# Tracing a routing step's row numbers and counts twelve steps later, and their stores three more

## The chip, the cores and the metric

One core of a Trainium2 chip runs the whole program. The metric is the time of one execution on the device in microseconds (us), taken outside the profiler; a profiled execution of the same kernel gives the trace. The engines are TensorE (PE), VectorE (DVE), ScalarE (ACT), GpSimd (POOL) and SyncE (SP), which here mostly issues DMAs. Each engine runs its instructions in the order in which the program holds them.

## The reference

Three layers follow each other. For 4 batches of 576 tokens, 8 heads of 64:

```python
def phi(x):                                # attention by 128 random features
    h = x @ omega.T - 0.5 * sum(x * x)
    return exp(h - max(h)) / sqrt(128)
kv  = einsum('bhsm,bhsd->bhmd', phi(k), v);  z = sum(phi(k), over s)
x   = einsum('bhsm,bhmd->bhsd', phi(q), kv) / (phi(q) . z + 1e-6)   # 2304 x 512

logits = x @ w_gate                        # 8 experts, w_gate 512 x 8
expert = argmax(logits);  gate = softmax(logits)[expert]
y = gate * (relu(x @ w1[expert]) @ w2[expert])       # 512 -> 1024 -> 512, one expert for a token

h = y @ w_in                               # 512 -> 2048
out = (h * sigmoid(1.702 * h)) @ w_out     # 2048 -> 512
```

## The kernel before, in words

The program goes over the batches. For each, the attention works in quads of four heads: k and q are loaded, transposed by DMA and multiplied by `omega` (`pr`); DVE takes row maxima (`small`), subtracts (`qp`, `kp`), ACT takes exponentials; `kv_ps` and `num` are the two products of the attention, and `xn` its normalized output. PE transposes `xn` (`tx`), and ACT and DVE split it into a high and a low part (`xh`, `xl`), since each exact fp32 product is made of three products of such parts. The attention of later batches is woven between the expert layer of earlier ones, so that the engines always have both kinds of work.

**Routing.** When a batch's attention is done, `route_steps(b)` runs. It makes the logits `lg`, their row maxima `rm`, a one-hot `oh`, exponentials `ex` and the gate. PE counts the one-hot over all tokens (`ct_ps`), and the expert with the largest count is `ci`, as an integer `es`. SP reads `es` into a register (`values_load`), and with it loads this one expert's weights (`st`) by DMA. The batch is then computed as if all its tokens went to this expert. ACT converts each piece of weights to its high part `wh`, and POOL (in places DVE) subtracts that for the low part `wl`. PE multiplies into PSUM tiles `m_ps`, of which there are two, ACT writes `h1h` from one and DVE `h1l`, and only then is its bank free for the next group of twelve products.

**The count.** The same function also does what is needed only if some token went to another expert: for each of the five blocks of 128 tokens a MAX (`lmx`) and a MAX_INDEX (`lix`) find the token's expert, `ixf` is that as a float, `cif` is the batch's expert as a float, `eq` compares the two, `hit` counts the agreements, `total` is lowered by them, and `rr` holds for each token an expert number and its gate, stored to `r_dram` by two DMAs on SP's queue. At the end of the program `total`, summed over the partitions on PE and cast to `tot_i`, decides whether a general path over `r_dram` runs. With these inputs it doesn't.

**Order.** The program is traced by Python generators that a merging loop advances in turn, so the text order is a weave; a scheduler then sets each engine's order by its own estimate of the times. The loop calls `tick()` once in each of its steps. `lag(n, fn)` puts `fn` off by n steps, and `flush()` calls all that is still waiting. `behind(ins, n)` keeps an instruction behind the n instructions that stand before it on its engine, without a wait.

After the four batches the last layer runs on PE nearly alone, its first weights having been prepared by DVE in between (`z`, from `raw_o`).

Of the kernel before, what the change touches and what calls it, by code (L numbers as in the profile page):

```python
# [8 lines left out]
F32 = mybir.dt.float32  # L9
# [3 lines left out]
U32 = mybir.dt.uint32  # L13
I64 = mybir.dt.int64
ACTF = mybir.ActivationFunctionType
ALU = mybir.AluOpType
AX = mybir.AxisListType
# [5 lines left out]
def kernel(  # L23
# [13 lines left out]
    nc = tc.nc  # L37
    B, H, S, D = q.shape
    M = omega.shape[0]
    E, DM, F1 = w1.shape  # L40
    F2 = w_in.shape[1]
    NT = B * S
    P = 128
    T = 4
    TAIL = S - T * P
# [63 lines left out]
    r_dram = dram.tile([NT, 2], F32, name="r_dram")  # L109
# [4 lines left out]
    def behind(ins, n):  # L114

        eng, me = ins.ins.engine, ins.ins.name
        found = [i for i in reversed(nc.cur_bb.bb.instructions) if i.engine == eng and i.name != me][:n]
        for x in found:
            tc.add_manual_dep(
                ins.ins, x.name,  # L120
                mybir.DependencyInfo(mybir.DependencyClass.NoSync, mybir.DependencyReason.DATA),
                reason="behind",
            )
# [44 lines left out]
    total = const.tile([P, 1], F32, name="total")  # L168
# [9 lines left out]
    def lag(n, fn):  # L178
        late.append((clock[0] + n, fn))
# [30 lines left out]
    att = tc.alloc_tile_pool(name="att", bufs=1)  # L210
# [289 lines left out]
    def route(b):  # L500
        g = route_steps(b)
        while True:
            with tc.high_priority() if b < HP_ROUTE else nullcontext():
                c = next(g, "end")
            if c == "end":
                return
            yield c

    def route_steps(b):
# [3 lines left out]
        for hf, tg in ((0, "n"), (1, "u")):  # L513
            c = slice(hf * HS, (hf + 1) * HS)
# [9 lines left out]
        for t in range(T + 1):  # L524
# [8 lines left out]
        lg = att.tile([P, T + 1, E], F32, tag="lg", name="lg", bufs=1)  # L533
# [10 lines left out]
            out=ex, in0=lg, in1=rm.to_broadcast([P, T + 1, E]), op=ALU.subtract  # L544
# [6 lines left out]
            out=ct_ps.rearrange("p t e -> p (t e)"), lhsT=ones, rhs=oh.rearrange("p t e -> p (t e)")  # L551
# [4 lines left out]
        ci = att.tile([P, 8], U32, tag="ci", name="ci", bufs=2)  # L556
# [4 lines left out]
        gate = att.tile([P, T + 1, 1], F32, tag="gate", name="gate", bufs=2)  # L561
# [4 lines left out]
        for t in range(T + 1):  # L566
            n = P if t < T else TAIL
            nc.scalar.activation(
                out=dg[:n, t * P:t * P + n], in_=ident[:n, :n], func=ACTF.Copy, scale=gate[:n, t, :]
            )  # L570
        cif = att.tile([P, 1], F32, tag="cif", name="cif", bufs=2)
        nc.vector.tensor_copy(cif, ci[:, 0:1])
        mx = att.tile([P, T + 1, 8], F32, tag="lmx", name="lmx", bufs=1)
        ix = att.tile([P, T + 1, 8], U32, tag="lix", name="lix", bufs=1)
        for t in range(T + 1):
            nc.vector.max(mx[:, t], lg[:, t])
            nc.vector.max_index(ix[:, t], mx[:, t], lg[:, t])
        ixf = att.tile([P, T + 1, 1], F32, tag="ixf", name="ixf", bufs=1)
        nc.vector.tensor_copy(ixf, ix[:, :, 0:1])
        eq = att.tile([P, T + 1, 1], F32, tag="eq", name="eq", bufs=1)  # L580
        nc.vector.tensor_scalar(out=eq, in0=ixf, scalar1=cif[:, 0:1], scalar2=None, op0=ALU.is_equal)
        nc.vector.memset(eq[TAIL:, T, :], 0.0)
        rr = att.tile([P, T + 1, 2], F32, tag="rr", name="rr", bufs=2)
        nc.vector.scalar_tensor_tensor(
            out=rr[:, :, 0:1], in0=eq, scalar=-float(2 * E), in1=ixf, op0=ALU.mult, op1=ALU.add
        )
        hit = att.tile([P, 1], F32, tag="hit", name="hit", bufs=1)
        nc.vector.tensor_reduce(out=hit, in_=eq.rearrange("p t o -> p (t o)"), axis=AX.X, op=ALU.add)
        nc.vector.tensor_tensor(out=total, in0=total, in1=hit, op=ALU.subtract)
        nc.vector.tensor_copy(rr[:, :, 1:2], gate)  # L590
        yield 0.5
        reg_t[b] = nc.values_load(
            es[0:1, 0:1], engines=[mybir.EngineType.SP], min_val=0, max_val=E - 1,
            skip_runtime_bounds_check_because="an index of the largest of E counts",
        )
        pump()
        nc.sync.dma_start(
            out=r_dram[b * S:b * S + T * P].rearrange("(p t) c -> p t c", t=T), in_=rr[:, 0:T]
        )
        nc.sync.dma_start(out=r_dram[b * S + T * P:(b + 1) * S], in_=rr[:TAIL, T])  # L600
        gb = moe.tile([P, S], F32, tag="gb", name="gb", bufs=2)
        g1 = pp.tile([P, T * P], F32, tag="u", name="g1", bufs=1)
        for t in range(T):
# [41 lines left out]
    def pump(n=0):  # L645
        ahead = 2 * NW - 1 if prep["split"] < 2 else NST
        while prep["staged"] < min(max(prep["split"] + ahead, 2 * NW - 1), 2 * NW * B) and prep["staged"] // (2 * NW) in reg_t:
            stage(*divmod(prep["staged"], 2 * NW))
            prep["staged"] += 1
        while n and prep["split"] < min(prep["free"], prep["staged"]):  # L650
            split_w(*divmod(prep["split"], 2 * NW))
            prep["split"] += 1
            n -= 1
# [310 lines left out]
    if True:  # L964
# [26 lines left out]
        while a_live:  # L991
            if force == "a" or (force is None and done_a - lead <= A_RATIO * done_m):
                c = next(A, "end")
# [5 lines left out]
            else:  # L999
                c = next(Mg)  # L1000
# [363 lines left out]
        p = hp.tile([P, SETW], F32R, tag="y2", name="p2", bufs=1)  # L1364
# [29 lines left out]
    with tc.If(more > 0), tc.tile_pool(name="gp", bufs=1) as gp:  # L1394
        with tc.For_i(0, NT // P, 1) as w:
# [21 lines left out]
            with tc.For_i(0, E, 1) as e:  # L1417
# [6 lines left out]
                with tc.If(cnt > 0):  # L1424
# [3 lines left out]
                    for f in range(NF1):  # L1428
                        wa = gp.tile([P, KD, P], F32, name="wa", bufs=2)
                        nc.sync.dma_start(  # L1430
                            out=wa,
                            in_=w1[bass.ds(e, 1), :, f * P:(f + 1) * P].rearrange(
                                "o (k p) f -> p (o k) f", p=P
                            ),
                        )
                        ps = pp.tile([P, P], F32, tag="m", name="g_ps", bufs=2)
                        for kk in range(KD):
                            nc.tensor.matmul(
                                out=ps, lhsT=wa[:, kk], rhs=xT[:, kk], start=(kk == 0), stop=(kk == KD - 1)
# [4 lines left out]
                    for dt in range(KD):  # L1444
                        wb = gp.tile([P, NF1, P], F32, name="wb", bufs=2)
                        nc.sync.dma_start(
                            out=wb,
                            in_=w2[bass.ds(e, 1), :, dt * P:(dt + 1) * P].rearrange(
                                "o (k p) d -> p (o k) d", p=P
                            ),  # L1450
                        )
                        ps = pp.tile([P, P], F32, tag="m", name="g_ps", bufs=2)
                        for f in range(NF1):
                            nc.tensor.matmul(
                                out=ps, lhsT=wb[:, f], rhs=ha[:, f], start=(f == 0), stop=(f == NF1 - 1)
# [53 lines left out]
```

## Time and profile before

| what | value |
|---|---|
| three runs | 767.16, 768.01, 770.99 us; median 768.01 us |
| the profiled execution | 765.51 us |
| its span in the trace | 763.5 us (the remaining 2.0 us lie ahead of and behind the recorded work) |
| busy: PE, DVE, ACT, POOL | 740.5, 533.3, 340.0, 132.3 us |
| granted clock of PE, mean | 0.995 of full speed |

Busy times are sums over one engine's instructions. An engine that is busy in nearly all of the span sets the time, if its work does not change; what it waits for in the rest is read from the waits and from the engines' rows in order of time.

### The profile page before, as it was taken

To read this page: it belongs to the slowest core of one execution; us is meant where nothing else is said; L and a number is where in the kernel's file an instruction comes from. 1 tells how busy PE (TensorE), PEld (TensorE's weight loads), DVE (VectorE), ACT (ScalarE), POOL (GpSimd) and SP (SyncE) were. 2 spreads that over 40 slices of the span, in tenths; PEclk is the share of its full clock that TensorE was granted. 3 is DMA by queue.
4 is the path that set the end of the run, shared out by engine and by line. 5 is a ranking of instruction groups with operands and counts; after the bars stand their busy time and mean duration, and the time that the engine had idled before them with its cause. 6 is when DMAs were issued, how large, how long until landed. Compare 5 with 4: busy or idle time off the path is not lost.

```text
span 763.5 us, 14425 instructions
## 1 busy us (share of the span) xinstructions
PE 740.5 (97%) x5589; PEld 717.1 (94%) x5589; DVE 533.3 (70%) x1188; ACT 340.0 (45%) x653; POOL 132.3 (17%) x78
## 2 busy tenths in 40 slices
PE   7998899999999999999999999999999999999997
PEld 6877799999999999989999999999999999999997
DVE  5877876686775686565979559981368777777774
ACT  5555573343533332233427564454576443444331
POOL 3564296538400441000000000000000000000000
PEclk9999899999999999999999999999999999999999
DMA  5447575258623553188255549972978544443311
GB/s 163 119 129 184 159 250 151 68 153 223 130 67 119 169 180 126 48 260 274 63 166 194 186 162 303 319 258 101 327 279 301 166 138 139 138 126 120 115 28 33
DMA packets 135852, 126.59 MB, mean 166 GB/s; under 512 B 57696, under 2 KB 120416, under 8 KB 134880
## 3 DMA queue, kind: packets, MB, share of 16 engines
q1 hardware_dynamic: 123936, 98.85, 43.6%
q10 hardware_dynamic: 11840, 26.74, 9.7%
q8 instruction: 46, 0.75, 0.4%
q14 instruction: 30, 0.25, 0.1%
HBM read 78.69 MB, written 40.39 MB: 156 GB/s over the span
## 4 chain that ended last, share of the span: by engine, by line
PE 82%; DVE 8%; DMA 4%; issue 3%; ACT 2%; SPq 1%; POOL 1%; ACTq 0%; POOLq 0%; DVEq 0%
PE m_ps L127 17%; PE qa L1213 13%; PE qa L1110 13%; PE qm L1213 7%; PE w_ps L127 4%; PE pb L1213 3%; PE qm L1110 3%; PE qu L1110 3%; PE num L433 3%; DMA st<-in_moe_w_dram 2%; PE kv_ps L391 2%; PE pr L333 2%; PE qn L1110 2%; PE qt L1110 2%; PE tq L419 1%
## 5 line engine op out<-in xcount | busy, mean ns | idle before, releaser
L1110 PE MATMUL qa<-y,wi 128*128 128x384 f32 x576 | 109.2, 337 | 0.4 <-DVE g L865 0.4
L1110 PEld LDWEIGHTS qa<-y,wi 128*128 128x128 f32 x576 | 101.4, 188 | 0.8 <-DVE g L865 0.8
L127 PE MATMUL m_ps<-xh,wh 128*128 128x288 f32 x256 | 78.5, 307 | 2.0 <-DVE h1l L699 2.0
L127 PE MATMUL m_ps<-xh,wl 128*128 128x288 f32 x256 | 76.1, 297 | 0.0
L127 PE MATMUL m_ps<-xl,wh 128*128 128x288 f32 x256 | 75.5, 295 | 0.0
L664 POOL TENSOR_TENSOR wl<-st,wh 128x1024 fp32r<-128x1024 f32 x23 | 55.6, 2424 | 92.7 <-ACT wh L662 87.5
L348 DVE TENSOR_REDUCE small<-pr 128x4 f32<-128x512 f32 (+1 forms) x80 | 51.1, 639 | 12.6 <-PE pr L340 5.0
L662 ACT ACTIVATE wh<-st 128x1024 fp32r<-128x1024 f32 (+1 forms) x33 | 33.9, 1033 | 53.3 <-DMA st<-in_moe_w_dram 37.4
L699 DVE SCALAR_TENSOR_TENSOR h1l<-m_ps,h1h 128x288 fp32r<-128x288 f32 x64 | 28.8, 452 | 33.2 <-ACT h1h L696 33.2
L127 PEld LDWEIGHTS m_ps<-xh,wh 128*128 128x128 f32 x256 | 48.1, 188 | 3.6 <-DVE h1l L699 3.2
L127 PE MATMUL m_ps<-h1h,wh 128*128 128x288 f32 x160 | 48.7, 305 | 0.7 <-DVE h1l L699 0.7
L127 PEld LDWEIGHTS m_ps<-xl,wh 128*128 128x128 f32 x256 | 48.1, 188 | 0.0
L127 PEld LDWEIGHTS m_ps<-xh,wl 128*128 128x128 f32 x256 | 48.1, 188 | 0.0
L696 ACT ACTIVATE h1h<-m_ps 128x288 fp32r<-128x288 f32 x64 | 25.7, 404 | 49.9 <-PE m_ps L127 47.6
L127 PE MATMUL m_ps<-h1l,wh 128*128 128x288 f32 x160 | 47.7, 299 | 0.0
L127 PE MATMUL m_ps<-h1h,wl 128*128 128x288 f32 x160 | 47.4, 297 | 0.0
L1213 PE MATMUL qa<-p,p 128*128 128x256 f32 x360 | 46.1, 282 | 1.1 <-DVE p L819 0.8
L1213 PE MATMUL qa<-p,gs 128*128 128x256 f32 x360 | 45.9, 282 | 0.0
L1213 PEld LDWEIGHTS qa<-p,p 128*128 128x128 f32 x360 | 44.1, 189 | 1.6 <-DVE p L819 1.0
L1213 PEld LDWEIGHTS qa<-p,gs 128*128 128x128 f32 x360 | 44.2, 189 | 0.0
L433 PEld LDWEIGHTS num<-kv,qpT 128*128 128x128 f32 (+1 forms) x320 | 36.2, 183 | 5.4 <-ACT qpT L421 2.7
L433 PE MATMUL num<-kv,qpT 128*128 128x65 f32 (+1 forms) x320 | 39.0, 265 | 2.3 <-ACT qpT L421 1.4
(212 smaller groups left out, 1830.7 us busy)
## 6 DMA issues: line engine op xcount, KB each, us to landing
g_dram<-g ACTq DMA_DIRECT2D x48, 384.0 KB, 3.9
st<-in_moe_w_dram SPq DMA_DIRECT2D x31, 512.0 KB, 4.6
pg<-g_dram SPq DMA_DIRECT2D x10, 1024.0 KB, 5.3
raw<-in_moe_w_in_dram SPq DMA_DIRECT2D x16, 512.0 KB, 3.9
gt<-g_dram SPq DMA_DIRECT2D x8, 1024.0 KB, 5.2
p<-wo_dram SPq DMA_DIRECT2D x6, 1024.0 KB, 7.1
yt<-y_dram SPq DMA_DIRECT2D x12, 384.0 KB, 5.9
vm<-in_v_dram SPq DMA_DIRECT2D x32, 128.0 KB, 3.0
```

Source lines behind the costliest of these rows:

```text
L127: ins = nc.tensor.matmul(out=ps, lhsT=a, rhs=b, start=start and n == 0, stop=stop and n == 2)
L333: nc.tensor.matmul(out=ps[:, :, h2], lhsT=xT[:, (2 * pr + h2) * 2 + t0 // 2], rhs=wbd)
L348: nc.vector.tensor_reduce(out=pm, in_=ps[:, :w], axis=AX.X, op=ALU.max, negate=on_act)
L391: nc.tensor.matmul(out=kv_ps[:, h, :], lhsT=kp[j // 2][:, j % 2, h2, :], rhs=vm[:, h, t, :], start=(t == 0), stop=False,)
L419: nc.tensor.transpose(tq[:, c, h2], qp[i][:, c, h2, :], ident)
L433: nc.tensor.matmul(out=ps[:n, c, h2, :], lhsT=lhsT, rhs=kv[:, h, :])
L662: nc.scalar.activation(out=hi[:, :, s], in_=st[:, :, s], func=ACTF.Copy)
L664: eng.tensor_tensor(out=lo[:, :, s], in0=st[:, :, s], in1=f32(hi)[:, :, s], op=ALU.subtract)
L696: nc.scalar.activation(out=hh[:, f], in_=ps, func=ACTF.Relu)
L699: nc.vector.scalar_tensor_tensor(out=hl[:, f], in0=ps, scalar=0.0, in1=f32(hh[:, f]), op0=ALU.max, op1=ALU.subtract)
L1110: ins = nc.tensor.matmul(out=ps, lhsT=w[:, a, ks], rhs=y[:, b, kk], start=start and kk + m == 0, stop=kk == 1 and m == 2, skip_group_check ...
L1213: ins = nc.tensor.matmul(out=ps, lhsT=x[:, f], rhs=w[i][:, f], start=start and f + m == 0, stop=f == NP - 1 and m == 2, skip_group_check=True,
```

## The change

In `route_steps(b)` the instructions from `cif` to the second column of `rr` move into a function `counted()`, which `lag(12, counted)` calls twelve steps later; the two stores to `r_dram` move into `rows()`, which is called three steps after that. `cif` and each MAX are kept behind the two DVE instructions that stand ahead of them where they are traced. No instruction is added or taken away, and `es`, the register load and the weights' DMAs stay.

```diff
-        cif = att.tile([P, 1], F32, tag="cif", name="cif", bufs=2)
-        nc.vector.tensor_copy(cif, ci[:, 0:1])
...
-        for t in range(T + 1):
-            nc.vector.max(mx[:, t], lg[:, t])
-            nc.vector.max_index(ix[:, t], mx[:, t], lg[:, t])
...
-        nc.vector.tensor_copy(rr[:, :, 1:2], gate)
         yield 0.5
         reg_t[b] = nc.values_load(
...
         pump()
-        nc.sync.dma_start(
-            out=r_dram[b * S:b * S + T * P].rearrange("(p t) c -> p t c", t=T), in_=rr[:, 0:T]
-        )
-        nc.sync.dma_start(out=r_dram[b * S + T * P:(b + 1) * S], in_=rr[:TAIL, T])
+
+        def counted():
+            cif = att.tile([P, 1], F32, tag="cif", name="cif", bufs=2)
+            behind(nc.vector.tensor_copy(cif, ci[:, 0:1]), 2)
...
+            for t in range(T + 1):
+                behind(nc.vector.max(mx[:, t], lg[:, t]), 2)
+                nc.vector.max_index(ix[:, t], mx[:, t], lg[:, t])
+            ixf = att.tile([P, T + 1, 1], F32, tag="ixf", name="ixf", bufs=1)
+            nc.vector.tensor_copy(ixf, ix[:, :, 0:1])
+            eq = att.tile([P, T + 1, 1], F32, tag="eq", name="eq", bufs=1)
+            nc.vector.tensor_scalar(out=eq, in0=ixf, scalar1=cif[:, 0:1], scalar2=None, op0=ALU.is_equal)
+            nc.vector.memset(eq[TAIL:, T, :], 0.0)
+            rr = att.tile([P, T + 1, 2], F32, tag="rr", name="rr", bufs=2)
+            nc.vector.scalar_tensor_tensor(
+                out=rr[:, :, 0:1], in0=eq, scalar=-float(2 * E), in1=ixf, op0=ALU.mult, op1=ALU.add
+            )
+            hit = att.tile([P, 1], F32, tag="hit", name="hit", bufs=1)
+            nc.vector.tensor_reduce(out=hit, in_=eq.rearrange("p t o -> p (t o)"), axis=AX.X, op=ALU.add)
+            nc.vector.tensor_tensor(out=total, in0=total, in1=hit, op=ALU.subtract)
+            nc.vector.tensor_copy(rr[:, :, 1:2], gate)
+
+            def rows():
+                nc.sync.dma_start(
...
+                nc.sync.dma_start(out=r_dram[b * S + T * P:(b + 1) * S], in_=rr[:TAIL, T])
+
+            lag(3, rows)
+
+        lag(12, counted)
```

Two places of the new order matter for what follows. The first is DVE behind the routing of batch 0, where the first groups of the expert layer run (`wl` and `h1l` are theirs; `rd`, `xn`, `xl`, `small`, `mx` and `qp` belong to the attention of the next batch). Before, these rows stood there:

```order
L438 RECIPROCAL rd<-rd 128x4
L444 TENSOR_TENSOR xn<-num,rd 128x2x128
L462 TENSOR_TENSOR xl<-small,xh 128x64
L699 SCALAR_TENSOR_TENSOR h1l<-m_ps,h1h 128x288 x2
L462 TENSOR_TENSOR xl<-tx,xh 128x512
L462 TENSOR_TENSOR xl<-small,xh 128x64
L348 TENSOR_REDUCE small<-pr 128x4
L357 TENSOR_TENSOR small<-small,sq 128x4
L357 TENSOR_TENSOR mx<-small,sq 128x4
L369 TENSOR_TENSOR qp<-pr,mx 128x512
L348 TENSOR_REDUCE small<-pr 128x4
L699 SCALAR_TENSOR_TENSOR h1l<-m_ps,h1h 128x288
```

Now the count stands among them. From the last MAX on the rows are (ahead of them, behind `xn`, stand `cif` and the other four pairs of MAX and MAX_INDEX):

```order
L584 MAX lmx<-lg 128x8
L707 SCALAR_TENSOR_TENSOR h1l<-m_ps,h1h 128x288
L585 MAX_INDEX lix<-lmx,lg 128x8
L587 CAST ixf<-lix 128x5
L589 TENSOR_SCALAR eq<-ixf,cif 128x5
L590 MEMSET eq 64x1
L707 SCALAR_TENSOR_TENSOR h1l<-m_ps,h1h 128x288
L592 SCALAR_TENSOR_TENSOR rr<-eq,ixf 128x5
L596 TENSOR_REDUCE hit<-eq 128x1
L462 TENSOR_TENSOR xl<-tx,xh 128x512
L462 TENSOR_TENSOR xl<-small,xh 128x64
L597 TENSOR_TENSOR total<-total,hit 128x1
```

The first `h1l` now has ten of the count's instructions ahead of it, and between the first and the third stand the last search, `ixf`, `eq` and its memset, `rr`, `hit` and `total`; behind `total` follow the reduction `small` and the other rows of before, up to the third `h1l`. The count came from the same engine's rows in batch 0's route, between the logits and `ct`, where these rows stood before:

```order
L543 TENSOR_TENSOR ex<-lg,rm 128x40
L577 MAX_INDEX lix<-lmx,lg 128x8
L576 MAX lmx<-lg 128x8 x4
L530 MEMSET lg_2056 128x16
L435 TENSOR_SCALAR rd<-num 128x4
L357 TENSOR_TENSOR small<-small,sq 128x2
L541 MEMSET oh 64x8
L577 MAX_INDEX lix<-lmx,lg 128x8 x2
L562 TENSOR_REDUCE gate<-ex 128x5
L577 MAX_INDEX lix<-lmx,lg 128x8 x2
L438 RECIPROCAL rd<-rd 128x4
```

From the two rows ahead of the same point (`ex`) on, the new order is:

```order
L348 TENSOR_REDUCE small<-pr 128x2
L540 TENSOR_TENSOR oh<-lg,rm 128x40
L543 TENSOR_TENSOR ex<-lg,rm 128x40
L435 TENSOR_SCALAR rd<-num 128x4
L357 TENSOR_TENSOR small<-small,sq 128x2
L541 MEMSET oh 64x8
L438 RECIPROCAL rd<-rd 128x4
L357 TENSOR_TENSOR mx<-small,sq 128x2
```

The MAX and MAX_INDEX are no longer among them. The second place is ACT at the end of the routing of batch 3, where `gb` is the gate, the table load and `wg<-total` prepare the last layer, and `wh_4380` is the first weight converted there. Before:

```order
L607 ACTIVATE gb<-g_3956 128x512
L608 ACTIVATE gb<-small 128x64
L926 DMA wo_dram<-z 128x4x256
L1014 ACT_TABLE_LOAD
L1014 ACTIVATE wg<-total 128x1
L908 DMA raw_o<-in_moe_w_out_dram 128x512 x2
L662 ACTIVATE wh_4380<-st 128x1024
L696 ACTIVATE h1h<-m_ps 128x288 x2
L662 ACTIVATE wh_4419<-st 128x1024
```

Now:

```order
L615 ACTIVATE gb<-g_3929 128x512
L616 ACTIVATE gb<-small 128x64
L934 DMA wo_dram<-z 128x4x256
L704 ACTIVATE h1h<-m_ps 128x288
L670 ACTIVATE wh_4380<-st 128x1024
L704 ACTIVATE h1h<-m_ps 128x288
L1022 ACT_TABLE_LOAD
L1022 ACTIVATE wg<-total 128x1
L916 DMA raw_o<-in_moe_w_out_dram 128x512 x2
L670 ACTIVATE wh_4419<-st 128x1024
```

One `h1h` has moved ahead of `wh_4380`, and the table load with `wg` has moved behind it. On DVE, `tot_i` stood between `total` and the first `wl` of that batch; now it stands behind that `wl` and one `h1l`. On SP the two `r_dram` stores stand a few issues later than before, in every batch.

## Rows read from the trace of the kernel before

**Rows 1.** The page's part 1, PE and the other engines: busy time, share, instructions.

```profile
PE 740.5 (97%) x5589; PEld 717.1 (94%) x5589; DVE 533.3 (70%) x1188; ACT 340.0 (45%) x653; POOL 132.3 (17%) x78
```

**Rows 2.** Busy time by stretch: PE, PEld, DVE, ACT, POOL, then PEclk, DMA, GB/s.

```profile
79.35:80.25 0.90, 0.15 (x4) 0.04 (x1) 0.90 (x4) 0.00 (x0) 0.90 (x1) 0.87 0.00 0
80.25:87.20 6.95, 6.20 (x39) 5.46 (x39) 6.44 (x48) 2.87 (x9) 0.36 (x1) 0.53 0.65 147
93.00:106.00 13.00, 13.00 (x110) 12.79 (x109) 8.28 (x21) 7.46 (x13) 9.43 (x4) 1.00 1.05 361
160.00:180.00 20.00, 20.00 (x170) 18.95 (x168) 12.20 (x37) 9.16 (x20) 10.71 (x6) 1.00 0.69 178
203.00:248.00 45.00, 45.00 (x394) 42.86 (x394) 29.08 (x112) 15.29 (x37) 2.37 (x1) 1.00 0.30 85
```

**Rows 3.** The chain that ended last, 78 to 110 us: start, length, piece.

```profile
79.43 0.08 DVE lmx L576
...
82.39 0.07 DVE ixf L579
...
82.94 0.62 PE ct_ps L550 x2
```

**Rows 4.** Timeline of SP's queue, 75 to 94 us: start, length, line, operation.

```profile
79.56 6.78 SPq L298 DMA_TRANSPOSE xT<-hl  x2
87.68 5.58 SPq L640 DMA_DIRECT2D st<-in_moe_w_dram  x8
```

**Rows 5.** Instructions on `lix`: duration in ns (min, median, max), first and last start.

```profile
L577 DVE FIND_INDEX8 lix<-lmx,lg x20: 154/161/171, 80.8 to 318.1; 128x8 uint32<-128x8 f32 x20
```

**Rows 6.** Timeline of ACT, 90.5 to 104 us, with idle time before in brackets.

```profile
90.66 1.19 ACT L662 ACTIVATE wh<-st 128x512 fp32r<-128x512 f32 x2
...
96.19 1.06 ACT L662 ACTIVATE wh<-st 128x1024 fp32r<-128x1024 f32 x1 [0.30 <-DMA st<-in_moe_w_dram]
97.15 0.39 ACT L696 ACTIVATE h1h<-m_ps 128x288 fp32r<-128x288 f32 x1
```

**Rows 7.** Timeline of PE, 90 to 108 us.

```profile
92.13 0.40 PE L127 MATMUL m_ps<-xh,wh 128*128 128x288 f32 x1
...
104.38 0.30 PE L127 MATMUL m_ps<-xh,wh 128*128 128x288 f32 x1
```

**Rows 8.** Timeline of DVE, 91 to 106 us.

```profile
95.92 0.23 DVE L462 TENSOR_TENSOR xl<-small,xh 128x64 fp32r<-128x64 f32 x1 [1.81 <-ACT xh L458]
97.58 0.46 DVE L699 SCALAR_TENSOR_TENSOR h1l<-m_ps,h1h 128x288 fp32r<-128x288 f32 x1 [1.43 <-ACT h1h L696]
99.03 0.46 DVE L699 SCALAR_TENSOR_TENSOR h1l<-m_ps,h1h 128x288 fp32r<-128x288 f32 x1 [1.00 <-ACT h1h L696]
...
102.72 0.45 DVE L699 SCALAR_TENSOR_TENSOR h1l<-m_ps,h1h 128x288 fp32r<-128x288 f32 x1
```

**Rows 9.** Timeline of POOL, 91 to 110 us.

```profile
95.85 9.51 POOL L664 TENSOR_TENSOR wl<-st,wh 128x1024 fp32r<-128x1024 f32 x4 [15.24 <-ACT wh L662]
```

**Rows 10.** `eq`: durations of all four; then DVE's timeline at batch 1.

```profile
L581 DVE TENSOR_SCALAR eq<-ixf,cif x4: 226/232/1682, 85.9 to 324.2; 128x5 f32<-128x5 f32 x4
...
163.80 1.68 DVE L581 TENSOR_SCALAR eq<-ixf,cif 128x5 f32<-128x5 f32 x1
...
166.25 1.41 DVE L584 SCALAR_TENSOR_TENSOR rr<-eq,ixf 128x5 f32<-128x5 f32 x1
```

**Rows 11.** Timeline of POOL at the same place.

```profile
163.07 2.38 POOL L297 TENSOR_TENSOR hl<-m,hl 128x1152 f16<-128x1152 f32 x1 [19.15 <-DVE cm L557]
165.53 2.11 POOL L256 TENSOR_TENSOR m<-m 128x1152 f32<-128x1152 f32 x1
```

**Rows 12.** Timeline of ACT and of PE at batch 3, 324 to 332 us.

```profile
325.29 1.28 ACT L1014 ACT_TABLE_LOAD   x1 [0.55 <-DVE hit L588]
...
328.41 1.06 ACT L662 ACTIVATE wh<-st 128x1024 fp32r<-128x1024 f32 x1 [1.62 <-DMA st<-in_moe_w_dram]
...
331.15 0.40 PE L127 MATMUL m_ps<-xh,wh 128*128 128x288 f32 x1 [0.66 <-DVE h1l L699]
```

More of the change, by code (lines that the diff above doesn't have):

```diff
@@ L570, in route_steps @@
             )
-        cif = att.tile([P, 1], F32, tag="cif", name="cif", bufs=2)
-        nc.vector.tensor_copy(cif, ci[:, 0:1])
-        mx = att.tile([P, T + 1, 8], F32, tag="lmx", name="lmx", bufs=1)
-        ix = att.tile([P, T + 1, 8], U32, tag="lix", name="lix", bufs=1)
-        for t in range(T + 1):
-            nc.vector.max(mx[:, t], lg[:, t])
-            nc.vector.max_index(ix[:, t], mx[:, t], lg[:, t])
[L578 to L585, printed above, removed]
-        )
-        hit = att.tile([P, 1], F32, tag="hit", name="hit", bufs=1)
-        nc.vector.tensor_reduce(out=hit, in_=eq.rearrange("p t o -> p (t o)"), axis=AX.X, op=ALU.add)
-        nc.vector.tensor_tensor(out=total, in0=total, in1=hit, op=ALU.subtract)
-        nc.vector.tensor_copy(rr[:, :, 1:2], gate)
         yield 0.5
@@ L596, in route_steps @@
         pump()
-        nc.sync.dma_start(
-            out=r_dram[b * S:b * S + T * P].rearrange("(p t) c -> p t c", t=T), in_=rr[:, 0:T]
-        )
-        nc.sync.dma_start(out=r_dram[b * S + T * P:(b + 1) * S], in_=rr[:TAIL, T])
+        def counted():
+            cif = att.tile([P, 1], F32, tag="cif", name="cif", bufs=2)
+            behind(nc.vector.tensor_copy(cif, ci[:, 0:1]), 2)
+            mx = att.tile([P, T + 1, 8], F32, tag="lmx", name="lmx", bufs=1)
+            ix = att.tile([P, T + 1, 8], U32, tag="lix", name="lix", bufs=1)
+            for t in range(T + 1):
[16 more added lines that the diff above has]
+                nc.sync.dma_start(
+                    out=r_dram[b * S:b * S + T * P].rearrange("(p t) c -> p t c", t=T), in_=rr[:, 0:T]
+                )
+                nc.sync.dma_start(out=r_dram[b * S + T * P:(b + 1) * S], in_=rr[:TAIL, T])
+            lag(3, rows)
+        lag(12, counted)
         gb = moe.tile([P, S], F32, tag="gb", name="gb", bufs=2)
```

## The prediction

> **What bounds the kernel now.** I read the page first: TensorE (PE) is busy for 97% of the span [rows 1], so the time moves only where PE waits, or where its clock is low. A table by stretches then shows where these places are. In 93 to 106 us and in 160 to 180 us PE is busy in every microsecond, while DVE has 8.28 of 13 and 12.20 of 20 [rows 2]. The weak place is 79 to 92 us, the routing of batch 0. PE does 0.15 us of work in the 0.90 us ahead of 80.25, and from 80.25 to 87.20 the granted clock is 0.53, about the lower level of 1.2 GHz [rows 2]. Last I read the chain of waits through that place, and DVE, ACT, POOL and PE in order of time around the place to which the change moves work. That the moved work is small is plain from its rows: the search for an index behind each MAX8 is 0.16 us [rows 5], the MAX8 about as long. The question is what each instruction waits for in its new place.
>
> **What leaves batch 0's route (79 to 93 us).** The chain goes through the count: from the first `lmx` at 79.43 to `ixf` at 82.39 there are seven pieces of it, 1.23 us in all, and behind them `xn` releases PE's `ct_ps` at 82.94 [rows 3]. Without them `ct_ps` and all behind it can start up to 1.2 us earlier. PE can't keep all of it, since the experts' weights bound what follows: SP's queue is in two transposing loads from 79.56 to 86.34, and the weights are issued from 87.68 [rows 4]. An earlier `es` passes neither. ACT converts the first two pieces of a weight from 90.66 for 1.19 us, so that the first is there at 91.26 [rows 6]; PE's first `m_ps` product stands at 92.13 [rows 7]. So the lead at 92 us is at most 0.9 us; call this term **-0.9** (0 to -0.9). The two stores of `rr` leave SP's queue from behind the weights' issues; nothing on PE reads what they write.
>
> **What arrives behind batch 0's route (94 to 105 us).** By the order rows, the count now follows `xn`, which ended at 94.1, and is mixed with the first two `h1l`. DVE idles 1.81, 1.43 and 1.00 us here [rows 8], 4.24 in sum. Five MAX8 and five searches at some 0.16 take 1.6 us and lie in the first two gaps, so they cost nothing as long as these gaps are there. The first `h1l` can't come earlier: it needs `h1h`, at 97.15 on ACT, and that stands behind a `wh` that begins at 96.19, when its weights land [rows 6]. So `h1l` ends at 98.04, the last search and `ixf` follow, and `eq` arrives at 98.2 to 98.5.
>
> There POOL is in the way. It runs four `wl` subtractions back to back from 95.85 for 9.51 us, 2.38 each, with ends at 98.2, 100.6, 103.0 and 105.4 [rows 9]. What POOL does to these small instructions is seen at batch 1: `eq` takes 1.68 us instead of its median 0.23 and ends at 165.48, `rr` takes 1.41 and ends at 167.66 [rows 10]; POOL's `hl` ends at 165.45, its `m` at 167.64 [rows 11]. Each came out as soon as POOL's instruction was over. `h1l`, which reads PSUM, isn't held: 0.46 us at 97.58 and at 99.03, both under `wl` [rows 8].
>
> So `eq` and `rr` each wait for an end of a `wl`; `total`, of a like form, has never met a POOL instruction in this trace. Four sums follow, by two open points.
> - `eq` gets through at 98.2, `rr` at 100.6. If `total` is held as well, to 103.0, what stands behind it by the order rows (two reductions, two small subtractions, `qp` and `h1l`, 2.8 us from the start of the first to the end of `h1l`, which is 103.17 today [rows 8]) put the end of the third `h1l` at 105.85. PE's fifth `m_ps` group needs the bank that it empties and starts at 104.38 today [rows 7]: **+1.5**. If `total` isn't held, +0.2.
> - `eq` misses 98.2 and gets through at 100.6, `rr` at 103.0. With `total` held to 105.4 the third `h1l` ends at 108.2: **+3.8**. Without, about 106.9: +2.5.
>
> PE runs its instructions in order and has the fifth group right behind the fourth, so this wait is lost; the lead from 92 us is eaten in it. The arrival is within 0.3 us of an end of a `wl`, which I can't settle, so I take the mean of the four, **+2.0**, and keep 0.2 to 3.8.
>
> The Trainium skill has this as a rule (SBUF — State Buffer, "Who interferes with whom"): DVE and GpSimd share one pair of SBUF ports as an exclusive lock, an instruction of DVE with two SBUF inputs contends with a GpSimd instruction that reads SBUF, and the one that comes second is fully blocked; one with at most one SBUF input outside the two-port modes is not. The held `eq` and `rr` and the free `h1l` agree with it. By this rule `total`, with two SBUF inputs, would be held too, and the term would be 1.5 or 3.8, with a mean of 2.65, and the time 770.4. No row of this trace shows `total` beside POOL.
>
> **Batch 1 (160 to 180 us).** The held `eq` and `rr` (1.45 and 1.25 us over their usual time) go from 163.8 to 167.7, and in their new place, some 4 to 10 us later, one or two of them probably wait for a `wl` again. PE had no idle time here with the hold [rows 2], so there is nothing to gain, and DVE has 7.8 us to spare in 20: **0** (-0.3 to +1).
>
> **Batch 2 (230 to 242 us).** From 203 to 248 us POOL has a single instruction of 2.37 us, DVE 29 of 45 us, and PE no idle time [rows 2]: **0**.
>
> **Batch 3 (323 to 332 us).** PE waits 0.66 us for `h1l` at 331.15, behind ACT's `wh` that waits 1.62 us for weights [rows 12]. In the new order one `h1h` more stands ahead of that `wh`, which can take away up to 0.66. Against it, the table load of 1.28 us, which lay in ACT's idle time at 325.29 [rows 12], now stands behind that `wh` and ahead of the next one. I take **-0.3**, between -0.7 and +0.6, the part of the load that its old cover leaves if half of it is uncovered.
>
> **Sum.** 765.5 (the profiled execution) + 2.0 + 0 + 0 - 0.3 = 767.2. The median of the runs is 768.0, 2.5 above the profiled one; with that, **769.7 us**.
>
> **Rivals.**
> - *Hidden.* `eq`, `rr` and `total` slip into the short gaps between two `wl`, or POOL's row of four has shifted, so that the third `h1l` ends by 104.3 as today. DVE's 4.24 us of idle time speak for it; against it, POOL's four stand without a gap [rows 9]. Then the lead of 0.9 stays: 768.0 - 0.9 - 0.3 = 766.8.
> - *Faster: the clock.* If the earlier `ct_ps` brings PE's full clock back early, or keeps it from falling, up to half of the 6.20 us of PE's work between 80.25 and 87.20 [rows 2] is won, 3.1 us, on top of the case before: 763.7. Against it: the clock falls at 80.25, when only one MAX8 of the count (0.08 us on the chain) has gone by. It decides if the fall is gone.
> - *Slower: a long stall and then the low clock.* `eq`, `rr` and `total` each wait for a `wl`, PE stands from 104.4 to 108.2, and the granted clock falls behind it as it did at 80.25, behind a stretch in which PE worked little. As the low stretch there cost 3.1 us, this gives 768.0 + 3.8 + 3.1 - 0.3 = 774.6. Against it: the stall ends before 106 in two of the four sums. It decides if PEclk falls anywhere behind 104.
>
> **Chances.** Held with a cost between 0.2 and 3.8: 0.50, its own range 767.9 to 771.5. Hidden: 0.20. Faster by the clock: 0.12. Long stall with low clock: 0.18. A measurement of this kernel can tell about 0.5%, 3.8 us, from no change: below 764.2 is faster, above 771.9 slower. The first case's upper end lies 0.4 below that bound and some of it (0.04) passes it. So faster 0.12, same 0.66, slower 0.22. The range leaves out the clock's gain and the upper part of the last case: 764.6 to 774.0.
>
> **What would show it.** Right: PE's `ct_ps` about 1.2 us earlier and `m_ps` at 91.3 to 92.1; `eq` and `rr` of batch 0 over 1 us long, each ending with a `wl`; PE idle 0.2 to 3.8 us for `h1l` near 104 to 108, at clock 1.00; at batch 1 no PE wait; less wait at 331. Wrong: `eq` and `rr` at 0.2 us near 98, or a PE wait in another place (a low clock behind 105, a later `wh` at batch 3).

## The result and the profile after

The changed kernel takes 777.71 us (median of six runs, 775.95 to 779.59) against 769.5 us of the kernel before on the same chip (six runs, 767.16 to 772.01): ratio 1.0105, 95% interval 1.0084 to 1.0127. It is slower by 8.2 us, outside the predicted range. One execution in a slower state, 786.45 us of the variant e7 below, is left out of all times and ratios. The page of the profiled execution (778.22 us) holds:

```profile
span 776.4 us, 14434 instructions
...
PE 743.2 (96%) x5589; PEld 719.4 (93%) x5589; DVE 541.3 (70%) x1188; ACT 340.4 (44%) x653; POOL 132.0 (17%) x78
```

PE's busy time rose by 2.7 us over [rows 1], though it runs the same 5589 products, and the span by 12.9 us over 763.5. That is more than the 8.2 us of the medians, since the profiled execution of before, 765.51 us, is one of its quick ones. Where the 12.9 us lie is seen in a table by stretches (PE, PEld, DVE, ACT, POOL, then PEclk, DMA share, GB/s) of after:

```profile
79.00:93.00 14.00, 11.67 (x111) 10.24 (x109) 12.79 (x59) 9.05 (x26) 1.55 (x2) 1.00 0.81 218
105.97:111.99 6.02, 6.02 (x35) 5.94 (x36) 4.35 (x14) 4.97 (x9) 3.04 (x2) 0.50 0.43 91
180.00:200.00 20.00, 15.78 (x125) 15.58 (x123) 11.04 (x34) 7.98 (x11) 12.34 (x6) 0.83 0.61 150
203.00:248.00 45.00, 45.00 (x408) 42.56 (x408) 31.25 (x101) 16.74 (x39) 4.78 (x2) 1.00 0.37 87
330.00:402.00 72.00, 66.60 (x489) 64.79 (x488) 49.30 (x108) 25.47 (x44) 0.00 (x0) 1.00 0.67 190
```

and of two of these stretches before:

```profile
180.00:200.00 20.00, 18.97 (x184) 17.95 (x184) 18.03 (x54) 10.58 (x19) 17.41 (x8) 1.00 0.78 194
330.00:402.00 72.00, 69.94 (x512) 68.98 (x512) 54.28 (x95) 24.62 (x42) 0.00 (x0) 1.00 0.59 183
```

**Batch 0.** The low clock of the routing, 0.53 in [rows 2], is gone in this execution (1.00 in 79 to 93). But then there is a new one, 0.50 for 6.02 us from 105.97. DVE's timeline ahead of it:

```profile
95.20 2.33 DVE L587 CAST ixf<-lix 128x5 f32<-128x5 uint32 x1
97.56 2.29 DVE L589 TENSOR_SCALAR eq<-ixf,cif 128x5 f32<-128x5 f32 x1
100.01 0.46 DVE L707 SCALAR_TENSOR_TENSOR h1l<-m_ps,h1h 128x288 fp32r<-128x288 f32 x1
100.38 1.92 DVE L592 SCALAR_TENSOR_TENSOR rr<-eq,ixf 128x5 f32<-128x5 f32 x1
103.02 0.15 DVE L597 TENSOR_TENSOR total<-total,hit 128x1 f32<-128x1 f32 x1
105.47 0.45 DVE L707 SCALAR_TENSOR_TENSOR h1l<-m_ps,h1h 128x288 fp32r<-128x288 f32 x1
```

POOL's at the same place:

```profile
92.79 9.49 POOL L672 TENSOR_TENSOR wl<-st,wh 128x1024 fp32r<-128x1024 f32 x4 [12.45 <-ACT wh L670]
```

and PE's:

```profile
89.38 0.38 PE L127 MATMUL m_ps<-xh,wh 128*128 128x288 f32 x1
...
90.57 0.40 PE L127 MATMUL m_ps<-xh,wh 128*128 128x288 f32 x1 [0.46 <-ACT wh L670]
...
105.97 0.61 PE L127 MATMUL m_ps<-xh,wh 128*128 128x288 f32 x1 [3.48 <-DVE h1l L707]
```

POOL's row is four subtractions of about 2.37 us, with ends near 95.2, 97.5, 99.9 and 102.3. `ixf`, `eq` and `rr` end at 97.53, 99.85 and 102.30: each was held until one of them was over. `h1l`, at 100.01 with 0.46 us under the last one, was not. The third `h1l` comes at 105.47, and PE begins its fifth group at 105.97 after 3.48 us without work: 1.59 later than in [rows 7], although its first `m_ps` product, at 89.38, was 2.75 earlier than there and the last product of the fourth group, at 102.20, still 2.05 earlier (before, 104.25). All of the place has moved: the first `h1l` stands at 94.56 in place of 97.58, POOL's row at 92.79 in place of 95.85. From the first `h1l` to the third it now takes 10.91 us, before 5.14. Behind the stall the clock is at its lower level, 1.2 GHz, for 6.02 us, which costs half of them, 3.0 us.

**Batch 1.** The chain that ended last (start, length, piece) shows the second place:

```profile
176.70 2.10 DVE ixf L587
...
179.95 0.16 DVE total L597
...
180.28 0.51 SPq L604
...
181.04 8.62 DMA st<-in_moe_w_dram
...
189.68 1.06 ACT wh L670
...
192.00 1.11 PE tq L419 x4
193.11 0.11 PE pr L339
...
199.27 0.06 PE pr L339
```

Here `ixf` takes 2.10 us (POOL's `wl` ends at 178.77), `rr` follows late, and the two stores of `rr` go out from SP's queue only at 179.88 and 180.28. Behind them stands the next weight, `st`. Its buffer came free at 178.77, with the end of that `wl`, but it is issued at 181.04, 2.27 us later, and lands 8.62 us after that. (Without the stores, in e4 below, the same load goes out 0.03 us behind the `wl`.) ACT converts it, `xl` stands on DVE behind ACT's `xh`, and PE waits 4.22 us (187.78 to 192.00). Then a `pr` product takes 0.11 us; at 199.27, with the clock back, 0.06. PE is busy for 15.78 us of 20 here, before for 18.97: 3.2 us lost by waiting. The low clock (0.50 from 192.00 to 195.24, 0.63 from there to 198.00) takes another 0.50 x 3.24 + 0.37 x 2.76 = 2.6 us.

**Batch 3.** PE is busy for 66.60 of 72 us, before for 69.94: 3.3 us lost, in four waits between 348 and 360 behind a weight that landed some 10 us after its issue at 340.37.

1.6 + 3.0 + 3.2 + 2.6 + 3.3 = 13.7 us, against 12.9 of the spans; a little comes back elsewhere (from 248 to 330 PE does 81.38 us of work, before 81.05). In 203 to 248 PE is busy throughout, as before.

### The profile page after: what moved, and what is told of

Its sections match the earlier page's. It is cut to its first block, busy times and chain, and to the rows that moved or that the text cites. A ratio compares the mean times of both kernels' runs of the same rounds, so it can differ in the third digit from the quotient of the medians.

```text
span 776.4 us, 14434 instructions
## 1 busy us (share of the span) xinstructions
PE 743.2 (96%) x5589; PEld 719.4 (93%) x5589; DVE 541.3 (70%) x1188; ACT 340.4 (44%) x653; POOL 132.0 (17%) x78
## 4 chain that ended last, share of the span: by engine, by line
PE 78%; DVE 9%; DMA 7%; ACT 2%; issue 2%; SPq 1%; POOL 0%; ACTq 0%; POOLq 0%; DVEq 0%
PE m_ps L127 16%; PE qa L1221 13%; PE qa L1118 13%; PE qm L1221 7%; DMA st<-in_moe_w_dram 5%; PE w_ps L127 3%; PE pb L1221 3%; PE qm L1118 3%; PE qu L1118 3%; PE num L433 3%; PE kv_ps L391 2%; PE qn L1118 2%; PE tq L419 2%; PE qt L1118 1%; PE pr L333 1%
```

## The experiments

Ratios are to the kernel before on the same chip, with 95% intervals. They need not equal the quotient of two medians, and the kernel before took 769.5, 768.95 (e1 to e4), 766.83 (e5 to e8) and 766.60 us (e9 to e12) beside them, so it is the ratios that can be compared. The experiments share one version of the changed function in which `LATE` holds the batches whose count is put off, `LAG_C` the steps for each, and `rows()` is called in the old place for the others; `LATE = (0, 1, 2, 3)` stands for the changed kernel, `LATE = ()` for the kernel before. An edit is shown against the changed kernel in this form. The scheduler sets the orders anew for each edit, so an edit can move more than it names; where the order of a trace decides a reading, it is said.

**One batch at a time.** The count and the stores late in batch 0, 1 or 3 alone:

```diff
-    LATE = (0, 1, 2, 3)
+    LATE = (0,)        # e1;  (1,) in e2;  (3,) in e3
```

> Only batch 0's count and stores are late; batches 1 to 3 as before. Theory (the loss has a part of its own in each batch): at batch 0 ixf, eq and rr are held by POOL's wl, PE waits some 3.5 us near 105 and then runs some 6 us at the half clock, while the half clock at 80 to 87 us is gone: in all 2 to 5 us slower than the kernel before, and no wait of PE for xl near 190. Rival (one cause, the late phase behind batch 0, brings the later waits with it): the wait near 190 comes as well, 6 us or more slower.

> Only batch 1's count and stores are late. Theory (the two r_dram stores wait on SP's queue for rr and hold the weights' issues behind them): PE waits 3 to 5 us near 183 to 190 for xl, behind a wh that waits for its weights; 3 to 7 us slower than before. Rival (batch 1 lost time in the full change only because batch 0 had shifted it): within 1 us of before.

> Only batch 3's count and stores are late. Theory (the raw_o loads of ACT's queue now stand behind a wh that waits for weights, land some 5 us later, and hold z, the next weights and h1l): PE loses 2 to 4 us between 330 and 402, 2 to 4 us slower than before. Rival (the loss there came from the shift of the earlier batches): within 1 us of before.

Measured: 777.02 us, 1.0111 (1.0081 to 1.0141) for batch 0; 770.58 us, 1.0028 (1.0009 to 1.0047) for batch 1; 770.36 us, 1.0021 (0.9996 to 1.0046) for batch 3. The parts do not add up: batch 0 alone loses all that the whole change loses, more than the 2 to 5 us expected, and without the wait near 190 that the rival asked for (PE is busy in all of 180 to 200). Its own stall is there (3.61 us for `h1l`, at 107.10), and a second one arises at batch 1, whose count stands where it stood before. DVE there:

```profile
169.69 1.79 DVE L586 TENSOR_SCALAR eq<-ixf,cif 128x5 f32<-128x5 f32 x1
171.64 2.02 DVE L589 SCALAR_TENSOR_TENSOR rr<-eq,ixf 128x5 f32<-128x5 f32 x1
174.25 1.72 DVE L594 TENSOR_TENSOR total<-total,hit 128x1 f32<-128x1 f32 x1
```

and POOL:

```profile
169.06 2.39 POOL L297 TENSOR_TENSOR hl<-m,hl 128x1152 f16<-128x1152 f32 x1 [20.65 <-ACT hl L296]
171.53 2.11 POOL L256 TENSOR_TENSOR m<-m 128x1152 f32<-128x1152 f32 x1
173.60 2.35 POOL L683 TENSOR_TENSOR wl<-st,wh 128x1024 fp32r<-128x1024 f32 x1
```

In [rows 10] the same `eq` and `rr` were held in the same way and cost nothing. Now the place comes 5.9 us later (169.69 for 163.80), POOL has a third instruction right behind the two, `total` is held too (each of the three ends with one of POOL's, at 171.5, 173.7 and 176.0), and PE waits 2.5 us for the `kp` behind it:

```profile
PE pr L339 <- DVE kp L369: 2.5, 1, 2.5
```

Behind this wait the clock is 0.50 from 177 to 183. So a hold that is free at one moment is not free at another, and a shift of one batch can bring it out in the next. Batch 1 alone showed a wait of 3.0 us for `xl` near 190 and clock 0.83 in 180 to 200, as in the whole change, but lost less than the 3 to 7 us expected. Batch 3 alone left PE busy for 67.65 of 72 us, and the third weight's conversion 7.0 us behind the second; the interval of its ratio holds 1. In that run's expectation I had named the order of the `raw_o` loads on ACT's queue as the cause; the next run keeps that order and not the loss, so that the order alone is not the cause.

**Without the stores.** The stores to `r_dram` are left out, in the changed kernel and in the kernel before (the general path, which doesn't run here, would find no rows):

```diff
-                lag(LAG_R, rows)      # e4, changed
...
-            rows()                    # e5, before
```

> The whole change, but the rows of expert numbers and gates are not stored (the general path, which does not run, would have nothing to read). Theory (stores hold SP's queue at batch 1): the wait of 4.2 us near 190 and the half clock behind it are gone or under 1 us, 4 to 6 us faster than the changed kernel, that is 2 to 4 us slower than before. Rival (POOL's hold of ixf and xl makes that wait, or the weights land late on their own): the wait stays at 3 to 5 us, 7 to 9 us slower than before.

> The kernel before without the stores of expert numbers and gates (left out as in the run of the whole change without them). Theory (the stores cost where they fall between a batch's weights, not as such; before, they stand right behind the first weights): 767 to 770 us, within 2 us of before. Rival (each pair of stores costs some us of DMA time wherever it stands): 4 to 8 us faster than before.

Measured: 767.67 us, 1.0001 (0.9983 to 1.0018), and 764.43 us, 0.9967 (0.9947 to 0.9987). With the changed kernel this makes a table of four (each against the kernel before on its own chip):

| | stores in their place | no stores |
|---|---|---|
| count and stores as before | 1 | 0.9967 |
| both late | 1.0105 | 1.0001 |

The right half of the second row is a clean comparison: up to 343 us DVE's instructions in e4 follow each other as in the changed kernel, but for one exchanged pair. So the late stores cost 1.0105 against 1.0001, some 8 us, as much as the whole loss; and this for 4 KB and 0.5 KB a batch, whose data no instruction of this run reads. The first row is not as clean. Up to 107 us e5 has DVE's order of before, from there on another; its `eq` and `rr` of batch 1, at 163.65 and 165.29, lie ahead of POOL's work (from 168.43) and are not held. So its 0.33% may be the order's, and what the stores cost in their old place is open. If it is 0.33%, two thirds of the loss come from the stores' new place; if it is nothing, all of it. Batch 0's stall is still there in e4 (3.6 us for `h1l`), but PE is busy in all of 180 to 200 and for 71.20 us in 330 to 402. In ACT's timeline at batch 3 the third weight of the list follows the second like this in the changed kernel:

```profile
340.81 1.04 ACT L670 ACTIVATE wh<-st 128x1024 fp32r<-128x1024 f32 x1
...
350.46 1.06 ACT L670 ACTIVATE wh<-st 128x1024 fp32r<-128x1024 f32 x1 [6.42 <-DMA st<-in_moe_w_dram]
```

and like this without the stores:

```profile
334.03 1.05 ACT L680 ACTIVATE wh<-st 128x1024 fp32r<-128x1024 f32 x1
...
338.43 1.06 ACT L680 ACTIVATE wh<-st 128x1024 fp32r<-128x1024 f32 x1 [1.17 <-DMA st<-in_moe_w_dram]
```

9.65 us against 4.40.

**The stores on another queue.** All stays as in the changed kernel, but ACT's queue issues the two stores. Is it SP's queue that stands still behind the stores (they wait for `rr`), or do the writes themselves hold the transfers up?

```diff
-            nc.sync.dma_start(out=r_dram...
+            nc.scalar.dma_start(out=r_dram...
```

> The whole change, with the two stores of each batch issued from ACT's queue in place of SP's. Theory (on SP's queue they wait for rr and hold the weights' issues and data behind them): PE's wait of 4.2 us near 190 is under 1.5 us and the time 768 to 773 us. Rival (the small stores themselves slow all DMA that is under way, whichever queue issues them): the wait stays at 3 us or more, 775 to 779 us.

Measured: 772.47 us, 1.0080 (1.0052 to 1.0108). The wait at batch 1 is gone (PE busy in all of 160 to 200). There the first load now goes out 0.02 us behind POOL's `wl` (which ends at 178.97), ahead of the first store, which ACT issues at 179.35:

```profile
178.99 0.38 SPq L659 DMA_DIRECT2D st<-in_moe_w_dram  x1
```

So it has neither the queue's wait nor the writes ahead of it, and this place doesn't tell the two apart; the next run does. At batch 3 the loss stayed (66.71 of 72). ACT issues the stores at 331.92 and 332.31 and two `raw_o` loads at 332.88 and 333.46, SP a weight at 334.19:

```profile
331.92 0.36 ACTq L599 DMA_DIRECT2D r_dram<-rr  x1
...
333.46 0.44 ACTq L927 DMA_DIRECT2D raw_o<-in_moe_w_out_dram  x1
...
344.08 1.06 ACT L681 ACTIVATE wh<-st 128x1024 fp32r<-128x1024 f32 x1 [6.50 <-DMA st<-in_moe_w_dram]
```

The view of the DMAs from 331.5 to 344 us has the bytes moved in 40 slices of 0.31 us, and below it the loads with their KB and the median us from issue to landing:

```profile
GB/s 184 23 23 13 13 0 2 0 39 39 223 13 0 0 0 13 131 79 26 26 13 105 249 419 420 420 419 446 364 357 406 354 338 351 354 370 357 226 89 69
raw_o<-in_moe_w_out_dram ACTq DMA_DIRECT2D x2, 512.0 KB, 7.4
st<-in_moe_w_dram SPq DMA_DIRECT2D x2, 512.0 KB, 9.1
```

From 334.2 on three loads of 512 KB are open on two queues, and yet little is moved until 338.1 but for a few slices; then they run at 340 to 450 GB/s. So loads issued behind these small stores waited for some 4 to 5 us, on SP's queue too, which held no store of `rr`.

**Larger rows.** Are the short rows the reason? Each store writes whole rows of 512 bytes, padded with zeros, to a wider tensor in DRAM, in the same place and waiting for the same `rr`:

```diff
-            rr = att.tile([P, T + 1, 2], F32, tag="rr", name="rr", bufs=2)
+            rr = rw_t[b][:, 0:2 * (T + 1)].rearrange("p (t c) -> p t c", c=2)
...
-            nc.sync.dma_start(out=r_dram[...], in_=rr[:, 0:T] ...)
+            nc.sync.dma_start(out=rw_dram[b * 2], in_=rw_t[b])
```

(`rw_t[b]` is 128x128 and zeroed by POOL beforehand; the second store is changed alike, and `r_dram` is not written.)

> The whole change with the same two stores at the same places on SP's queue, still waiting for rr, but each partition's row is padded to 512 bytes (the general path, which does not run, would have to read them at other addresses). Theory (writes of 8 and 32 bytes hold up the transfers behind them for some us): the weights land about 5 us after their issue behind the stores, as without stores, PE's wait near 190 is under 2 us, and the time is 768 to 772 us. Rival (SP's queue, which waits for rr, is what holds the weights): the wait near 190 and the loss between 330 and 402 stay, 775 to 779 us.

Measured: 770.44 us, 1.0035 (1.0013 to 1.0058), two thirds of the loss gone with 16 and more times the bytes; DVE's order is that of the changed kernel but for a few exchanged neighbours. SP's queue waits as before: POOL's `wl` ends at 182.42, and the load goes out behind the stores 2.22 us later (2.27 in the changed kernel), lands 5.41 us after that in place of 8.62, and PE waits 1.1 us for `xl` in place of 4.2:

```profile
183.91 0.48 SPq L605 DMA_DIRECT2D rw_dram<-rr  x1
184.64 0.40 SPq L662 DMA_DIRECT2D st<-in_moe_w_dram  x1
```

and among PE's waits (total, times, longest):

```profile
PE tq L420 <- DVE xl L463: 1.1, 1, 1.1
```

So of the 4.2 us the queue's wait alone leaves 1.1. In 330 to 402 PE is busy for 70.73 us of 72. The DMAs of the 6.5 us behind the first store at batch 1, in the changed kernel:

```profile
GB/s 0 17 9 0 0 1 2 0 0 0 63 101 164 227 50 0 0 0 0 0 0 0 0 0 6 132 170 57 25 13 25 25 0 25 32 57 158 227 221 284
st<-in_moe_w_dram SPq DMA_DIRECT2D x2, 512.0 KB, 8.8
```

and with the wide rows:

```profile
GB/s 0 0 161 230 13 0 66 133 3 0 76 221 246 132 145 239 246 403 277 290 347 364 299 330 339 364 365 340 378 372 365 381 347 301 109 60 113 139 365 391
st<-in_moe_w_dram SPq DMA_DIRECT2D x2, 512.0 KB, 5.1
```

Weights land in 8.8 us behind the short rows and in 5.1 behind the wide ones; in the corresponding 6.5 us without stores (e4) in 3.8. The Trainium skill (DMA: Bandwidth & Descriptors, Specifications) has 512 bytes as the least transfer for full rate and says that a smaller one is a read, a change and a write. The runs agree in so far as rows padded to this length hold the loads behind them less, 5.1 against 8.8 us; no other length was tried, and no run shows the read and the change. Why the short rows hold up others, and not only themselves, is open.

**A quiet place for batch 0's count, then for batch 1's too.** If the hold by POOL is what costs at batch 0, a place without POOL gives the gain of the shorter route without the stall.

```diff
-    LATE = (0, 1, 2, 3);  LAG_C = (12, 12, 12, 12)
+    LATE = (0,);          LAG_C = (60, 12, 12, 12)     # e7
+    LATE = (0, 1);        LAG_C = (60, 45, 12, 12)     # e8
```

> Only batch 0's count and stores are late, and by 60 steps in place of 12, so that they fall into the stretch near 130 to 160 us where GpSimd has nothing to do; batches 1 to 3 as before. Theory (late is good for batch 0's route, and only POOL's hold at 95 to 105 spoils it): ixf, eq, rr and total at 0.15 to 0.25 us each, no wait of PE near 105, full clock at 80 to 87 and at 105 to 112; 2 to 5 us faster than before. Rival (any later place loses, since DVE, ACT and DMA of the next route are pressed): the time stays within 2 us of before or above it.

> As the run with batch 0's count 60 steps late, and batch 1's 45 steps late as well (it falls behind 200 us, where GpSimd is idle too). Theory: the hold of eq and rr at batch 1 (2.7 us of DVE before) goes as well; PE had no wait there, so it is the same as the other within 1.5 us, 2 to 5 us faster than before. Rival (what stands behind batch 1's route decides): PE waits near 180 to 190 for xl or kp, and the time is 3 us or more above the other.

Measured: 780.44 us, 1.0154 (1.0077 to 1.0231; three runs, 773.44, 780.44 and 783.41) for batch 0 alone, 764.16 us, 0.9980 (0.9959 to 1.0001) for both. The first is the opposite of what was expected; the second is, by its interval, hardly told apart from the kernel before. In both the count of batch 0 stands near 150 us and is not held. In e8 POOL has no instruction from 148 to 158, and DVE shows:

```profile
152.21 0.16 DVE L584 CAST ixf<-lix 128x5 f32<-128x5 uint32 x1
152.41 0.23 DVE L586 TENSOR_SCALAR eq<-ixf,cif 128x5 f32<-128x5 f32 x1
```

PE is busy in all of 160 to 200 there, at clock 1.00, and for 70.51 of 72 in 330 to 402; the longest wait for `h1l` is 0.9 us. e7, which left batch 1's count in the old place, is slower than the change itself. Its longest waits of PE:

```profile
PE w_ps L127 <- ACT h1h L715: 7.9, 3, 3.9
PE pr L339 <- DVE kp L369: 2.0, 1, 2.0
```

The 2.0 us for `kp` lie behind batch 1's count, which is partly held by POOL again, as in e1. The 7.9 us for `h1h` lie at 296, 334 and 364 us and are not settled: weights that land late stand ahead of the first two, and stores in the old place beside the second, but which shift brought them together was not tried.

**The hold taken away where it arose.** The stores are left out as in e4, and DVE makes the low parts of batch 0's first five weights instead of POOL:

```diff
-    SPLIT_D = (0,)
+    SPLIT_D = (0, 1, 2, 3, 4)
```

> The whole change without the stores (left out), and with batch 0's first five weight pieces subtracted on DVE in place of GpSimd, so that nothing runs on GpSimd where batch 0's count stands. Theory (GpSimd holds ixf, eq and rr): these take 0.15 to 0.25 us each, and PE's wait of 3.6 us for h1l near 105 falls below 2 us (DVE has some 5 us more to do there); 762 to 768 us. Rival (the count's mere place between the first h1l makes the wait): it stays above 3 us, 768 us or more.

Measured: 764.29 us, 0.9976 (0.9957 to 0.9995), against 1.0001 of e4: taking POOL away at batch 0 gives 0.25%, 1.9 us, about as much as the two intervals together leave open; the traces are plainer. DVE and POOL at the place of the count:

```profile
102.57 0.17 DVE L584 CAST ixf<-lix 128x5 f32<-128x5 uint32 x1
103.85 1.17 DVE L586 TENSOR_SCALAR eq<-ixf,cif 128x5 f32<-128x5 f32 x1
105.60 0.17 DVE L589 SCALAR_TENSOR_TENSOR rr<-eq,ixf 128x5 f32<-128x5 f32 x1
```

```profile
102.62 2.37 POOL L682 TENSOR_TENSOR wl<-st,wh 128x1024 fp32r<-128x1024 f32 x1 [21.95 <-ACT wh L680]
```

`ixf` began 0.05 us ahead of POOL's subtraction and takes 0.17 us; `eq`, which meets it, is held to its end at 104.99; `rr` behind it is free. PE waits 1.1 us in place of 3.6, and its clock stays at 1.00 from 79 to 112.

**The best of both.** The count of batches 0 and 1 in the quiet places, and `rr` kept in SBUF for all batches and stored only inside the general path (e11); and the kernel before with the latter alone (e12). Both compute all of the reference.

```diff
-            rr = att.tile([P, T + 1, 2], F32, tag="rr", name="rr", bufs=2)
+            rr = rr_c[b]                  # one tile for each batch
...
-        rows()                            # per batch
...
+            for b in range(B):            # in the general path only
+                nc.sync.dma_start(out=r_dram...[b], in_=rr_c[b]...)
```

> Batches 0 and 1 with the count 60 and 45 steps late, batches 2 and 3 in place, and the rows kept in SBUF for all batches and stored only inside the general path, so that nothing of the reference is left out. Theory: the two gains add up, -2.5 us for the stores and -1.5 to -2.5 for the route without count: 0.4% to 0.8% faster than before. Rival (both gains are the same slack): not below the kernel before without stores, 0.2% to 0.4% faster than before.

> The kernel before, with the rows kept in SBUF and stored only inside the general path; nothing of the reference is left out. As the run of before without stores: 0.2% to 0.5% faster than before. Rival (that gain was the new order that the scheduler made, not the stores): within 0.15% of before.

Measured: 763.46 us, 0.9957 (0.9939 to 0.9975), and 764.51 us, 0.9986 (0.9965 to 1.0007). e11 is the fastest kernel of the study, 0.43% or 3.3 us below the kernel before. The interval of e12 holds 1, and its 0.14% is what the rival had said; e5, which leaves out the same stores and has the same order on DVE, gave 0.9967, and both have another order than the kernel before. So it is not shown that the stores cost anything in their old place. The intervals of e11 and e12 overlap too: that the two gains add up is not shown.

## Why the prediction was wrong

The forecast, 769.7 us, was 8 us too low; 1.5 of them are the kernel before itself, which took 769.5 us beside the changed one and not 768.0. Of a loss of 8.2 us it had 1.7.

- **"The two stores ... nothing on PE reads what they write."** This step failed, and it is most of the error. The sentence is true, and it asks the wrong question. What counts is what the stores wait for and what stands behind them. In their new place they wait on SP's queue for a late `rr` (at batch 1 the weight's buffer came free at 178.77, and its load was issued at 181.04), and the loads behind them land late (8.62 us). Without the stores, in the same order on DVE, all of the loss is gone (e4); with rows of 512 bytes, the queue's wait unchanged, two thirds of it (e9).
- **Batch 1, "0", and batch 3, "-0.3".** Measured 3.2 + 2.6 us and 3.3 us in the trace. Both came out of the step above: without stores these places lose nothing (e4). I had argued from PE's full row in [rows 2] that there was nothing to gain, and had looked for a loss only on DVE.
- **Batch 0's lead, "at most 0.9", and "the first `h1l` can't come earlier".** Both failed. The lead was 2.75 us at the first `m_ps` product and 2.05 at the end of the fourth group, and the first `h1l` came 3.02 earlier. I had taken SP's two transposing loads as fixed at 6.78 us [rows 4]; now they took 5.10 (why was not tried), the weights were issued from 85.76 in place of 87.68, and ACT's first `wh` began at 88.59 in place of 90.66. It waited 0.43 us for its weight, so the weights do bound the place, as written, but at another time. The lead was eaten by the stall.
- **Batch 0's hold, "+2.0", between 0.2 and 3.8.** The fifth group came 1.59 later: inside, but in part by luck. From the first `h1l` to the third the hold added 5.8 us (10.91 for 5.14), more than the worst of the four sums, and 3.0 us of earlier start, which I had excluded, hid the rest. It was also put together otherwise. Three instructions were held, as in the first of the four sums, but `ixf`, `eq` and `rr`, not `eq`, `rr` and `total`. The step "the last search and `ixf` follow" had `ixf` as free; no row of before showed it beside POOL. `total` fell behind POOL's last subtraction here; beside POOL in e1 it took 1.72 us. The Trainium skill (SBUF — State Buffer, "Who interferes with whom") names casts among the operations that can take the shared ports: by that, `ixf` can be held as well, and the trace agrees (2.33 us). The prediction had used only the half of the rule on two inputs.
- **The low clock behind the stall.** In the likeliest case it had no price; it was 3.0 us at batch 0 and 2.6 at batch 1. The rival "a long stall and then the low clock" named the mechanism with 3.1 us and a chance of 0.18. It put the stall's end at 108.2 and held against itself that it would end before 106; it ended at 105.97, and the clock fell all the same. The price isn't fixed: in the 6 us behind a stall of 3.6 us the clock was 0.72 in e1, e4 and e9, which costs 1.7 us.
- **"Faster: the clock."** Its condition came true: the low clock of 80 to 87 us is gone. In the same run the other rival took more than that back. The two had been written as alternatives, with one chance each, and they are not. But the fall at 80.25 doesn't hang on the count alone. With batch 0's count in its old place the clock in 80.25 to 87.20 was 0.53 before, and 0.67, 0.84, 1.00 and 0.82 in e2, e3, e5 and e12; with it late it was 1.00 in the changed kernel and six of the variants, and 0.75 in e7 and e9.
- **Batch 2, "0"**, was right (45.00 of 45).

## What to carry to other kernels

A DMA whose data nobody reads still stands in a queue and can hold up the loads behind it: before moving one, look at what it waits for, at which loads are issued behind it and in how short rows it writes. Small work on DVE moved out of a chain needs a place where GpSimd is idle, or forms that GpSimd doesn't hold, as `h1l` here; a hold that is free in one place says nothing of the next, and the place itself moves when something earlier does. On PE, 97% busy, a stall of some 3.5 us had a second price, the low clock behind it: 1.7 to 3.0 us in these traces.

## What the runs showed that I had not expected

- Stores of 4 KB and 0.5 KB, in rows of 32 and 8 bytes, held up loads issued behind them: 8.8 us to landing in place of 3.8 without them and 5.1 with rows of 512 bytes; and this also where the stores and the load stood on different queues (9.1 us at batch 3 in e6).
- A cast of 128x5 elements, 0.16 us alone, takes 2.33 us beside a POOL subtraction.
- After 3.48 us without work PE ran for 6.02 us at 1.2 GHz, after 4.22 us for some 5.
- The parts of a change do not add up: the whole cost 1.05%, batch 0's part alone 1.11%, and batch 0's part in a place without POOL 1.54% (0.77% to 2.31%). The last is open.
